# Attention beside a linear branch on one core: the keys' normaliser put on the values, the first 512 tokens turned by TensorE, 130 instead of 128 packs of exponentials off ScalarE

## The chip, the cores and the metric

One core of one Trainium2 chip. The metric is the device time of one execution in microseconds (us), as the median of several runs.

## The reference, cut to what matters

```python
# x [1, 2048, 512], H = 32 heads, Dh = 16; all inputs bf16
def branch_A(x, wqkv, wo):                      # softmax attention
    q, k, v = heads(x @ wqkv)
    p = softmax(q @ k.T * Dh ** -0.5)
    return merge(p @ v) @ wo

def branch_B(x, wqkv, w_phi, wo):               # linear attention
    q, k, v = heads(x @ wqkv)
    pq, pk = q @ w_phi, k @ w_phi               # per head, 16 x 16
    phi_q = concat(softmax(pq), softmax(-pq))   # 32 features
    phi_k = concat(softmax(pk), softmax(-pk))
    kv, z = phi_k.T @ v, phi_k.sum(over the tokens)
    o = (phi_q @ kv) / (phi_q @ z + 1e-6)
    return merge(o) @ wo

g = sigmoid((x * gate_w).sum(-1))
out = g * branch_A(x, A_wqkv, A_wo) + (1 - g) * branch_B(x, B_wqkv, B_w_phi, B_wo)
```

## The kernel before

Everything stays in SBUF; tokens are turned once into `xT` (512 features on the partitions, 2048 tokens along the free axis). A **group** `g` is one chunk `qc` of 512 queries and one of eight sets `g8` of four heads, of the 32, and it runs over the 16 tiles `kt` of 128 keys. One group and one key tile are a **pack** of four **units**, one for each head: a unit is the score matrix of one head, 128 keys by 512 queries, made by one matmul of 32 rows (L1022). There are 32 x 16 = 512 packs, 2048 units.

Most units have their exponential taken by ScalarE (ACT): `_exp` (L1070) reads two or three units in turn (1024 or 1536 columns) from a ring of five PSUM banks and writes bf16 into one of 30 slots of `ET`; the `k`-th scores wait for exponential `k - 2`, whose banks they use. `_pv` multiplies a pack's four tiles by the values (L1135, four column tiles of TensorE side by side) and adds them up in a PSUM bank over the 16 key tiles.

The other packs go **away** from ACT: `AWAY` holds five bits for each group, and each bit set takes one of five key tiles (1, 4, 7, 10, 13) of that group. For such a pack VectorE (DVE) turns each unit's scores into the bits of a bf16 power of two (`_vector_bits`, L940, 512 columns a time), two more terms of the same bits are made by adding a shift on DVE (`_vector_terms`, L962, for two packs at a time with 4096 columns, or a single one with 2048) and a third on POOL (`_pool_term`, L977, two for each pack), and all four terms are multiplied by the values (`vc` is the values times a factor). So a pack away costs ACT nothing, and TensorE four value products where the others take one.

Branch B and the projections run beside this. `_b_fuse` folds `w_phi` into the weights. For the keys (`_b_quad` with `s = 1`, four **quads** of four token tiles) DVE evicts the features' logits (L1279), takes maxima and minima over the 16 features by a tree, subtracts them, ACT takes the exponentials of both signs (L1308), DVE sums them, and `_b_scale` takes one reciprocal of all 256 sums (L1329) and multiplies both halves of the features (L1330, twice). `_b_v` projects branch B's values and copies them from PSUM into `VB` with a column of ones behind every four heads (L1266), and `_b_kv` multiplies features by values and adds into `kvacc` (260 columns: 4 x 65). The queries' quads follow (`s = 0`: two reciprocals' worth of work as a ratio, L1334 to L1336), then the products with `kvbd` and the output projections. The query branch needs only the ratio of its two sums, because one common factor per token and head cancels in `num / den`.

The order of the work is not written by hand. Every piece is an `Op` on an engine with a planned cost, a priority `prio` and sometimes an earliest place `rel`, and `Plan.order` builds, ahead of time, one fixed queue for each engine by simulating them; `emit` turns the dependences into semaphore waits. `SHIFT` is a table of tags ("e3" for the projection of values in `_b_v` of tile 3, "d4" a quad, "p101" a pack) with an offset added to that tag's priority. On the chip each engine follows its queue in order and waits where a semaphore isn't there yet.

The start: SP issues DMA transposes of `x` (`_turn`, L1390; first two halves of 256 tokens, then three chunks of 512), ACT's queue issues three pieces of the weights (L525). TensorE meanwhile runs nine matmuls on a constant tile (`_warm`, L639). Then come k of the first 256 tokens (L662), q of both halves (L713, evicted twice with a mask by DVE, L719), k of the other half, the first scores and the first exponential. At the end the last packs' values, their normalisation, the output projection and the store follow the last exponential.

Of the kernel before, what the change touches and what calls it, by code (L numbers as in the profile page):

```python
# [6 lines left out]
ACT = mybir.ActivationFunctionType  # L7
# [3 lines left out]
P = 128  # L11
D = 512
H = 32
DH = 16
# [372 lines left out]
class _Kernel:  # L387
# [43 lines left out]
    def _memory(self, ctx):  # L431
# [42 lines left out]
        self.VB = sb("VB", [P, 4, 8, 65], BF16)  # L474
# [5 lines left out]
        self.kvacc = sb("kvacc", [P, 2, 260], F32)  # L480
# [29 lines left out]
    def _loads(self):  # L510
# [18 lines left out]
        for half in range(2):  # L529
            load_x(0, QCH // 2 * half, QCH // 2 * (half + 1), 4.1)  # L530
            self.b_x0[half].writers = self.b_xT[0].writers[half:]
# [17 lines left out]
    def _consts(self):  # L549
# [20 lines left out]
        self.o_vbones = op("POOL", lambda e: e.memset(self.VB[:, :, :, 64:65], 1.0), 0.3, prio=-20)  # L570
# [25 lines left out]

    def _projections(self):
# [11 lines left out]
        self._warm(9)  # L609
# [25 lines left out]
    def _warm(self, n):  # L635

        def run(e):
            for _ in range(n):
                ins = e.matmul(self.ps[:, 4, :], self.warm[:, 0:P], self.warm, start=True, stop=True)  # L639
            return ins  # L640
        self.plan.op("PE", run, 0.427 * n, reads=[self.b_warm], name="warm", prio=-99)
# [63 lines left out]
    def _proj_q0(self, half, bank):  # L705
# [41 lines left out]
    def _gate(self):  # L747
# [44 lines left out]
    AWAY = (22, 27, 28, 19, 26, 15, 29, 27, 27, 15, 15, 30, 31, 13, 15, 27, 15, 23, 31, 27, 27, 31, 31, 31, 26, 31, 25, 31, 30, 15, 19, 31)  # L792

    SHIFT = (
# [752 lines left out]
```

## Time and profile before

| what | us |
|---|---|
| median of 3 runs (lowest, highest) | 743.38 (743.01, 743.54) |
| profiled execution, its own time | 743.37 |
| its span | 741.6 |
| busy: PE, DVE, ACT, POOL | 710.9, 693.9, 727.0, 279.7 |

The span is the time from the first to the last instruction of the profile; the execution's own time also holds what lies around it. PE is TensorE, PEld its weight loads, DVE is VectorE, SP the engine that issues most DMAs. L1070 is line 1070 of the kernel. The row of a group of instructions gives its count, its busy time in total, the mean time of one in ns, and the idle time of the engine ahead of it with what ended it. A row of waits gives the total, the number of times and the longest. A row of the chain gives start, length and what ran. Matmul times are modelled, so a busy TensorE isn't one at its peak.

### The profile page before, as it was taken

What the parts mean: (1) busy time and instruction counts of PE and PEld (TensorE: products, weight loads), DVE (VectorE), ACT (ScalarE), POOL (GpSimd) and SP (SyncE); (2) the same over time, 40 slices, a digit from 0 to 9 for tenths busy, and PEclk for the clock granted to TensorE, in tenths of its full rate; (3) what the DMA queues carried; (4) which work ended last, traced back from release to release, by engine and by line L of the source; (5) the groups of instructions that cost most, each with busy time, mean ns of one, the idle gap of its engine ahead of it and who ended that gap; (6) DMA issues with size and microseconds to landing.
All of it is one profiled execution on the core that took longest, in us unless ns stands there. A gap on an engine that the chain in (4) does not pass through costs nothing.

```text
span 741.6 us, 19810 instructions
## 1 busy us (share of the span) xinstructions
PE 710.9 (96%) x8580; PEld 232.8 (31%) x8599; DVE 693.9 (94%) x1097; ACT 727.0 (98%) x635; POOL 279.7 (38%) x277
## 2 busy tenths in 40 slices
PE   8999999999999999999998999999999999999998
PEld 4334333333232322322222223322323233322322
DVE  5889989988999999999999999999999999999996
ACT  6999999999999999999999999999999999999996
POOL 4631331423434335232434344245342433325342
PEclk9999999999999999999999999999999999999999
DMA  9400000000000010000101301131211320231110
GB/s 201 142 12 14 12 2 13 13 4 13 14 9 11 3 22 8 9 9 8 16 8 20 55 14 32 30 76 13 31 23 30 51 44 8 39 81 20 23 23 30
DMA packets 90040, 21.96 MB, mean 30 GB/s; under 512 B 82912, under 2 KB 89440, under 8 KB 89952
## 3 DMA queue, kind: packets, MB, share of 16 engines
q1 hardware_dynamic: 88224, 20.17, 14.5%
q8 instruction: 67, 1.10, 0.6%
q10 hardware_dynamic: 1728, 0.52, 0.3%
q14 instruction: 21, 0.17, 0.1%
HBM read 4.21 MB, written 2.10 MB: 9 GB/s over the span
## 4 chain that ended last, share of the span: by engine, by line
ACT 89%; PE 6%; DVE 2%; DMA 1%; SPq 0%; issue 0%; DVEq 0%
ACT ET L1070 85%; ACT bq L1308 4%; PE ps L1022 2%; PE ps L1135 2%; PE ps L646 2%; DVE va L940 1%; DVE vp L962 1%; DMA xT<-in_A_x_dram 1%; DMA WT<-nb 1%; PE ps L736 0%; DVE bq L1279 0%; DVE nb L1420 0%; SPq L1390 0%; ACT xT L1496 0%; DVE rb L1418 0%
## 5 line engine op out<-in xcount | busy, mean ns | idle before, releaser
L1070 ACT ACTIVATE ET<-ps 128x1536 bf16<-128x1536 f32 x615 | 699.8, 1372 | 5.2 <-PE ps L1022 4.9
L977 POOL TENSOR_SCALAR vp<-va 128x1024 uint16<-128x1024 uint16 x260 | 271.8, 1045 | 450.4 <-DVE va L940 137.7
L940 DVE TENSOR_SCALAR va<-ps 128x512 uint16<-128x512 f32 x512 | 335.2, 684 | 25.1 <-PE ps L1022 22.0
L1022 PE MATMUL ps<-qT,kT 32*128 32x512 bf16 x2048 | 311.6, 384 | 20.3 <-ACT ET L1070 15.9
L1022 PEld LDWEIGHTS ps<-qT,kT 32*128 32x128 bf16 x2048 | 81.0, 91 | 265.9 <-ACT ET L1070 165.3
L962 DVE TENSOR_SCALAR vp<-va 128x4096 uint16<-128x4096 uint16 (+1 forms) x143 | 159.4, 1123 | 0.6 <-PE ps L1135 0.4
L1135 PE MATMUL ps<-ET,V 128*32 128x512 bf16 x1536 | 148.4, 385 | 1.4 <-DVE T L1156 1.3
L1135 PE MATMUL ps<-vp,vc 128*32 128x512 bf16 x1024 | 93.3, 384 | 0.3 <-DVE vp L962 0.3
L646 PE MATMUL ps<-WB,xT 128*32 128x512 bf16 x768 | 57.9, 382 | 0.0
L1135 PEld LDWEIGHTS ps<-ET,V 128*32 128x32 bf16 x1536 | 39.3, 95 | 57.1 <-issue 40.7
L1142 PE MATMUL ps<-kT,zero 128*32 128x512 bf16 x552 | 50.1, 385 | 0.4 <-ACT ET L1070 0.3
L1135 PE MATMUL ps<-va,V 128*32 128x512 bf16 x512 | 50.2, 385 | 0.0
L1135 PE MATMUL ps<-vp,V 128*32 128x512 bf16 x512 | 47.1, 384 | 0.7 <-DVE vp L962 0.7
L646 PE MATMUL ps<-xT,WA 128*32 128x512 bf16 x480 | 36.1, 382 | 0.3 <-DVE va L940 0.3
L1135 PEld LDWEIGHTS ps<-vp,vc 128*32 128x32 bf16 x1024 | 24.4, 95 | 35.9 <-issue 24.9
L1308 ACT ACTIVATE bq<-bq 128x2048 bf16<-128x2048 bf16 x16 | 32.7, 2046 | 0.0
L1156 DVE STREAM_TRANSPOSE T<-ps 128x512 f32<-128x512 f32 x32 | 22.7, 709 | 1.7 <-PE ps L1135 1.7
L646 PE MATMUL ps<-WoA,onTA 128*32 128x512 bf16 x256 | 23.2, 383 | 0.0
L646 PE MATMUL ps<-WoB,WT 128*32 128x512 bf16 x256 | 23.0, 383 | 0.0
L1279 DVE CAST bq<-ps 128x512 bf16<-128x512 f32 x32 | 21.8, 683 | 1.1 <-PE ps L646 1.1
L646 PEld LDWEIGHTS ps<-WB,xT 128*32 128x32 bf16 x768 | 15.6, 95 | 19.0 <-issue 11.2
L1135 PEld LDWEIGHTS ps<-va,V 128*32 128x32 bf16 x512 | 13.3, 95 | 20.4 <-issue 16.6
(86 smaller groups left out, 357.9 us busy)
## 6 DMA issues: line engine op xcount, KB each, us to landing
turned<-T SPq DMA_DIRECT2D x240, 8.0 KB, 1.8
qT<-qs SPq DMA_DIRECT2D x120, 16.0 KB, 1.8
WB<-in_B_wqkv_dram SPq DMA_DIRECT2D x1, 1536.0 KB, 6.9
out_dram<-WB SPq DMA_DIRECT2D x12, 128.0 KB, 1.9
WA<-in_A_wqkv_dram SPq DMA_DIRECT2D x3, 384.0 KB, 6.1
WoA<-in_A_wo_dram SPq DMA_DIRECT2D x1, 512.0 KB, 7.9
WoB<-in_B_wo_dram SPq DMA_DIRECT2D x1, 512.0 KB, 8.8
WA<-in_A_wqkv_dram ACTq DMA_DIRECT2D x3, 128.0 KB, 3.6
```

The costliest lines, as they stand in the source:

```text
L646: ins = e.matmul(out[32 * g:32 * g + 32], lhs[:, 32 * g:32 * g + 32], rhs, start=start, stop=stop, tile_position=(0, 32 * g), skip_group_c ...
L940: parts.append(op("DVE", lambda e, j=j, job=job: e.tensor_scalar(self.va[:, pair, side, j, :], self._bank(job), SCALE * LOG2E * 128.0, (12 ...
L962: self.plan.op("DVE", lambda e, k=k, shift=shift: e.tensor_scalar(flat(self.vp[:, k]), flat(self.va[:, pair]), float(shift), None, op0=ALU ...
L977: o = self.plan.op("POOL", lambda e, flat=flat: e.tensor_scalar(flat[0], flat[1], 1.0, float(shift), op0=ALU.mult, op1=ALU.add), 0.08 + n ...
L1022: return e.matmul(out, self.kT[32 * i:32 * i + 32, cp, kt * TOK:(kt + 1) * TOK], self.qT[32 * i:32 * i + 32, s, :], start=True, stop=True, ...
L1070: o = plan.op("ACT", lambda e: e.activation(self.ET[:, a % NS:a % NS + n, :], self.ps[:, self._ring(a):self._ring(a) + n, :], ACT.Exp, sca ...
L1135: ins = e.matmul(self._bank(ot)[32 * i:32 * i + 32, :], V[:, v0:v0 + 32], tile(), start=(kt == 0), stop=(kt == self.NT - 1), tile_position ...
L1142: ins = e.matmul(self._bank(ot)[32 * i:32 * i + 32, :], self.zero[:], self.kT[:, 0, 0:QCH], start=False, stop=False, tile_position=(0, 32 ...
L1156: self.turned_out = op("DVE", lambda e: e.transpose(T1[:, side].rearrange("p b s -> p (b s)"), src()), 0.635, deps=last, writes=[b_T1[side ...
L1279: [lambda e, b, k=k: e.tensor_copy(bq[:, k].rearrange("p (g s v) -> p g s v", g=8, s=2)[:, :, 0, :], b.rearrange("p (g v) -> p g v", g=8))],
L1308: op("ACT", lambda e, side=side: e.activation(sides[side], sides[side], ACT.Exp, scale=1.0 - 2 * side), self.c_act(2048) + 0.04, reads=[bu ...
```

## The change

1. **Keys' normaliser.** For the keys' quads the sums of the negative side get one reciprocal (128 columns), written straight into the 17th column of each head in `VB` (now 8 x 68 columns a tile, 17 for each head). A ratio of the two sums and a second reciprocal scale the positive features alone (one L1330-like product instead of two). The eviction of the values in `_b_v` becomes a product with that column, which takes the place of the ones; it, its matmuls and the `kv` products now wait for the new buffer `b_vr`, and the value projections are due later (`GAP * 10.2` into the quad). `kvacc` has 272 columns.
2. **First tokens.** The first 512 tokens come by four plain loads into `ET` slots 20 to 23 and are turned by TensorE (`_first_tokens`): four transposes for each 128 tokens, copied from PSUM into `xT` by DVE (first and third) and ACT (second and fourth). The warming matmuls go from nine to four, with one more after the second and the fourth turn. The masked q of the second half for one side is evicted by ACT instead of DVE.
3. **130 packs.** `AWAY` has 130 bits set instead of 128, in other places, and `SHIFT` is another table.

The diff, with the table `SHIFT` and lines around left out:

```diff
--- before.py
+++ after.py
@@ -471,13 +471,13 @@
-        self.VB = sb("VB", [P, 4, 8, 65], BF16)
+        self.VB = sb("VB", [P, 4, 8, 68], BF16)
...
-        self.kvacc = sb("kvacc", [P, 2, 260], F32)
+        self.kvacc = sb("kvacc", [P, 2, 272], F32)
@@ -526,9 +526,8 @@
-        for half in range(2):
-            load_x(0, QCH // 2 * half, QCH // 2 * (half + 1), 4.1)
-            self.b_x0[half].writers = self.b_xT[0].writers[half:]
+        self.x0 = [self.dma("SP", f"x{t}", lambda e, t=t: e.dma_start(
+            self.ET[:, 20 + t], self.x2d[TOK * t:TOK * t + TOK, :]), cost=0.45, prio=-60 + t, lat=2.3) for t in range(4)]
...
-        self.o_vbones = op("POOL", lambda e: e.memset(self.VB[:, :, :, 64:65], 1.0), 0.3, prio=-20)
...
+    def _first_tokens(self):
+
+        op = self.plan.op
+        for t in range(4):
+            job, pool = self._job(t if t < 2 else None)
+
+            def turn(e, t=t, job=job):
+                for c in range(4):
+                    ins = e.transpose(self._bank(job).bitcast(BF16)[:, P * c:P * c + P], self.ET[:, 20 + t, P * c:P * c + P], self.iden[:])
+                return ins
+            m = op("PE", turn, 4 * self.c_pe(128), reads=[self.b_iden], deps=[self.x0[t]], name="xtr", prio=-90 + t,
+                   acquire=pool)
+            if t % 2:
+                self._warm(1, [m])
+            out = self.xT[:, :, TOK * t:TOK * t + TOK]
+            src = lambda job=job: self._bank(job).bitcast(BF16)[:, 0:QCH].rearrange("p (c j) -> p c j", c=4)
+            if t % 2:
+                o = op("ACT", lambda e, out=out, src=src: e.activation(out, src(), ACT.Copy), self.c_act(QCH), deps=[m],
+                       name="xtr_ev", prio=-90 + t, release=pool)
+            else:
+                o = op("DVE", lambda e, out=out, src=src: e.tensor_copy(out, src()), self.c_dve(QCH), deps=[m],
+                       name="xtr_ev", prio=-90 + t, release=pool)
+            if pool is None:
+                self.early[t] = o
+            self.b_x0[t // 2].writers.append(o)
+        self.b_xT[0].writers = self.b_x0[0].writers + self.b_x0[1].writers
+
...
-        self._warm(9)
+        self._warm(4)
+        self._first_tokens()
...
-    def _warm(self, n):
+    def _warm(self, n, deps=()):
 
         def run(e):
             for _ in range(n):
                 ins = e.matmul(self.ps[:, 4, :], self.warm[:, 0:P], self.warm, start=True, stop=True)
             return ins
-        self.plan.op("PE", run, 0.427 * n, reads=[self.b_warm], name="warm", prio=-99)
+        self.plan.op("PE", run, 0.427 * n, reads=[self.b_warm], deps=deps, name="warm", prio=-99)
 
...
-            o = op("DVE", lambda e, side=side: e.tensor_scalar(
-                self.qT[:, side, at], self._bank(job)[:, 0:QCH // 2], self.mask[:, side:side + 1], None, op0=ALU.mult),
-                self.c_dve(256), reads=[self.b_mask], deps=[m], name="qproj_ev", prio=-40 + 70 * side,
-                release=pool if side else None)
+            if half and not side:
+                o = a = op("ACT", lambda e: e.activation(
+                    self.qT[:, 0, at], self._bank(job)[:, 0:QCH // 2], ACT.Copy, scale=self.mask[:, 0:1]),
+                    self.c_act(256), reads=[self.b_mask], deps=[m], name="qproj_ev", prio=-40)
+            else:
+                o = op("DVE", lambda e, side=side: e.tensor_scalar(
+                    self.qT[:, side, at], self._bank(job)[:, 0:QCH // 2], self.mask[:, side:side + 1], None,
+                    op0=ALU.mult), self.c_dve(256), reads=[self.b_mask], deps=[m, a if half else None], name="qproj_ev",
+                    prio=-40 + 70 * side, release=pool if side else None)
...
-    AWAY = (22, 27, 28, 19, 26, 15, 29, 27, 27, 15, 15, 30, 31, 13, 15, 27, 15, 23, 31, 27, 27, 31, 31, 31, 26, 31, 25, 31, 30, 15, 19, 31)
+    AWAY = (29, 29, 22, 13, 15, 27, 19, 23, 31, 15, 15, 31, 25, 23, 31, 15, 23, 27, 27, 15, 23, 23, 31, 31, 21, 31, 30, 31, 23, 15, 13, 31)
 
     SHIFT = (
...
     )
 
...
-        self.b_brec = B()
+        self.b_brec, self.b_vr = B(), B()
...
         for t in range(0, NT, 4):
             due = self.K0 + self.SK * t
+            of(f"d{t}", self._b_quad, 1, t, due)
             for k in range(4):
-                of(f"e{t + k}", self._b_v, t + k, due + self.GAP * k)
-            of(f"d{t}", self._b_quad, 1, t, due)
+                of(f"e{t + k}", self._b_v, t + k, due + self.GAP * 10.2 + k)
             of(f"a{t}", self._b_kv, t, due + 12 * self.GAP)
...
     def _b_v(self, t, due):
-        if t < 4:
-            self.b_VB[t].writers = [self.o_vbones]
+        heads = self.VB[:, t % 4].rearrange("p g (i v) -> p (g i) v", v=17)
         self._proj(lambda c: self.xT[:, c, TOK * t:TOK * t + TOK], lambda c: self.WB[:, c, 2 * D:3 * D],
-                   [self.b_xT[t // 4], self.b_WB],
-                   [lambda e, b: e.tensor_copy(self.VB[:, t % 4, :, 0:64], b.rearrange("p (g v) -> p g v", g=8))],
-                   self.c_dve(512), due + 4, due - 3, "bv", [self.b_VB[t % 4]])
+                   [self.b_xT[t // 4], self.b_WB, self.b_vr],
+                   [lambda e, b: e.tensor_tensor(heads[:, :, 0:16], b.rearrange("p (h d) -> p h d", d=DH),
+                                                 heads[:, :, 16:17].to_broadcast([P, 32, DH]), ALU.mult)],
+                   self.c_dve(512), due, due - 3, "bv", [self.b_VB[t % 4]])
 
...
+        pos, neg, r = total[:, 0::2], total[:, 1::2], r[:, 0:32]
         if s:
-            half = [slice(0, 32), slice(32, 64)]
-            return [("b_rec", 1.66, self._low(lambda e: e.reciprocal(r, total)), tree, b_r)] + [
-                ("b_mul", two(2048), lambda e, h=h: e.tensor_tensor(x[:, h], x[:, h], spread(r[:, h], 32), ALU.mult),
-                 b_r + both, both if h.start else [Buf()]) for h in half]
-
-        pos, neg, r = total[:, 0::2], total[:, 1::2], r[:, 0:32]
+            col = self.VB[:].rearrange("p t g (i v) -> p (t g) i v", v=17)[:, :, :, 16]
+            return [("b_rec", 0.86, self._low(lambda e: e.reciprocal(col, neg)), tree, [self.b_vr]),
+                    ("b_ratio", 0.2, lambda e: e.tensor_tensor(pos, pos, col, ALU.mult), tree + [self.b_vr], tree),
+                    ("b_rec", 0.86, self._low(lambda e: e.reciprocal(r, pos)), tree, b_r),
+                    ("b_mul", two(2048), lambda e: e.tensor_tensor(x[:, 0::2], x[:, 0::2], spread(r, 32), ALU.mult),
+                     b_r + both, [both[0]])]
+
...
-                        ins = e.matmul(self._bank(job)[:, 65 * g4:65 * g4 + 65],
+                        ins = e.matmul(self._bank(job)[:, 68 * g4:68 * g4 + 68],
...
-            m = op("PE", mm, 16 * self.c_pe(65), reads=self.b_bq[0:2] + self.b_VB, name="kv", prio=due, acquire=job)
+            m = op("PE", mm, 16 * self.c_pe(68), reads=self.b_bq[0:2] + self.b_VB + [self.b_vr], name="kv", prio=due, acquire=job)
...
-            acc = self.kvacc[:, hf, :].rearrange("p (g v) -> p g v", g=4)
+            acc = self.kvacc[:, hf, :].rearrange("p (g i v) -> p g i v", g=4, i=4)
...
```

More of the change, by code (lines that the diff above doesn't have):

```diff
@@ L1357, in mm @@
                 return ins
-            m = op("PE", mm, 16 * self.c_pe(65), reads=self.b_bq[0:2] + self.b_VB, name="kv", prio=due, acquire=job)
+            m = op("PE", mm, 16 * self.c_pe(68), reads=self.b_bq[0:2] + self.b_VB + [self.b_vr], name="kv", prio=due, acquire=job)
             acc = self.kvacc[:, hf, :]
             if t == 0:
-                op("DVE", lambda e, acc=acc, job=job: e.tensor_copy(acc, self._bank(job)[:, 0:260]), self.c_dve(260),
+                op("DVE", lambda e, acc=acc, job=job: e.tensor_copy(acc, self._bank(job)[:, 0:272]), self.c_dve(272),
                    deps=[m], writes=[self.b_kv[hf]], name="kvacc", prio=due, release=job)
             else:
-                op("DVE", lambda e, acc=acc, job=job: e.tensor_tensor(acc, acc, self._bank(job)[:, 0:260], ALU.add),
-                   self.c_dve(260), deps=[m], reads=[self.b_kv[hf]], writes=[self.b_kv[hf]], name="kvacc", prio=due,
+                op("DVE", lambda e, acc=acc, job=job: e.tensor_tensor(acc, acc, self._bank(job)[:, 0:272], ALU.add),
+                   self.c_dve(272), deps=[m], reads=[self.b_kv[hf]], writes=[self.b_kv[hf]], name="kvacc", prio=due,
                    release=job)
```

4 lines of the change are left out of this document (2 added, 2 removed), and 200 rows, old and new, of the table SHIFT.

## The prediction

> **What bounds the kernel now.** I read the engine totals first, then what ScalarE waited for, then the chain of waits at both ends of the run.
>
> ```profile
> span 741.6 us, 19810 instructions
> ## 1 busy us (share of the span) xinstructions
> PE 710.9 (96%) x8580; PEld 232.8 (31%) x8599; DVE 693.9 (94%) x1097; ACT 727.0 (98%) x635; POOL 279.7 (38%) x277
> ```
>
> Three engines are over 90% busy, so the totals alone don't name the bound. What ScalarE (ACT) waited for does:
>
> ```profile
> ACT ET L1070 <- PE ps L1022: 4.9, 2, 4.7
> ACT xT L1496 <- PE ps L646: 4.2, 1, 4.2
> ACT L1070 <- issue: 2.3, 1, 2.3
> ACT ET L1070 <- PE ps L1135: 0.2, 1, 0.2
> ```
>
> This is the whole list. The 4.7 is the wait for the first scores, the 4.2 the wait before the last two evictions; in between ACT was held up for some 0.4 us in all. The chain of waits at the start, and the row of the timeline with the last exponentials:
>
> ```profile
> 0.74 1.35 SPq L1390
> 2.14 4.49 DMA xT<-in_A_x_dram
> 6.67 0.61 PE ps L713 x4
> 7.29 0.44 PE ps L662 x4
> 7.95 0.35 PE ps L1022 x3
> 8.32 31.77 ACT ET L1070 x28
> 40.19 72.52 ACT ET L1070 x64
> ```
>
> ```profile
> 725.05 8.38 ACT L1070 ACTIVATE ET<-ps 128x1024 bf16<-128x1024 f32 x8
> ```
>
> So the run has three parts: a start of 8.32 us (the second half of the first 512 tokens lands at 6.63, its q projection, masking and first scores follow), a gapless file of ACT work from 8.32 to 733.43, and a tail of 8.2 us to 741.6. The profiled execution took 743.37, that is 1.77 outside the span; the median of the three runs is 743.38, so profile and median agree and I sum against 743.37. A change shortens the run by what it takes off the start, off ACT's own work, or off the tail; DVE and PE count only where they make ACT wait.
>
> **ACT's work: fewer exponentials.** The counts of ones in the two AWAY tuples of the diff are 128 and 130 packs; a pack is four units of 128x512 scores. ACT keeps 4 x (512 - 128) = 1536 units before, 1528 after, in alternating instructions of three and two units.
>
> ```profile
> L1070 ACT ACTIVATE ET<-ps 128x1536 bf16<-128x1536 f32 x307 | 486.2, 1584 | 5.2 <-PE ps L1022 4.9 <-PE ps L1135 0.2
> L1070 ACT ACTIVATE ET<-ps 128x1024 bf16<-128x1024 f32 x307 | 357.0, 1163 | 0.0
> L1308 ACT ACTIVATE bq<-bq 128x2048 bf16<-128x2048 bf16 x16 | 32.7, 2046 | 0.0
> L1070 ACT ACT_TABLE_LOAD x1 | 1.3, 1283 | 2.3 <-issue 2.3
> L1496 ACT ACTIVATE xT<-ps 128x512 bf16<-128x512 f32 x2 | 1.1, 596 | 4.2 <-PE ps L646 4.2
> L1070 ACT ACTIVATE ET<-ps 128x512 bf16<-128x512 f32 x1 | 0.7, 707 | 0.0
> ```
>
> The means 1584 and 1163 overlap with their neighbours (their sum is 2.75); what a pair really takes is its pitch, 72.52 / 32 = 2.266 us by the longest piece of the chain. Before: 307 pairs and one single unit, 307 x 2.266 + 0.71 = 696.4. After: 1528 = 305 x 5 + 3, so 305 pairs and a last instruction of three, 305 x 2.266 + 1.58 = 692.7. **Saved: 3.7 us.** The sixteen L1308 stay. The two evictions of the first tokens and one masked q that move to ACT stand ahead of the first exponential, where ACT idles anyway.
>
> **The start.** Gone are two DMA transposes; instead SP issues four plain loads of 128 tokens (128 KB each), TensorE turns each in four 128x128 transposes into PSUM, and DVE (tokens 0 and 2 of the four groups) or ACT (1 and 3) copies it out. Nothing before shows that load, so I bound it by two issues of the same size:
>
> ```profile
> WA<-in_A_wqkv_dram ACTq DMA_DIRECT2D x3, 128.0 KB, 3.6
> out_dram<-xT SPq DMA_DIRECT2D x3, 128.0 KB, 1.9
> ```
>
> ```profile
> 0.74 1.55 ACTq L525 DMA_DIRECT2D WA<-in_A_wqkv_dram  x3
> ...
> 1.45 4.02 PE L639 MATMUL ps<-bq 128*128 128x512 bf16 x9 [1.45 <-DVE bq L572]
> ```
>
> The weights land 3.6 us after issue, cut into 256-byte pieces and beside other loads; the stores of whole 1 KB rows land after 1.9 in a quiet stretch. The new loads have the rows of the second and the crowd of the first: I take 2.5. At 1.55 / 3 = 0.52 per issue the fourth is issued at 0.74 + 3 x 0.52 = 2.3 and lands at 4.8 (4.2 to 5.9 by the two rows). Its turn is half as many columns as the four matmuls of L662 (0.44), at most 0.4 with its way to PSUM; its copy by ACT is L1496's shape, 0.6; two semaphores, 0.1. The last q projection (L713 at 6.67) then starts at 5.9, 0.8 earlier. Ahead of it on PE stand the k and q projections of the first 256 tokens, 0.44 each: the second load lands at 1.26 + 2.5 = 3.8, is turned and copied by 4.9, and both are through by 5.8, just in time. From L713 to the first exponential it took 8.32 - 6.67 = 1.65; the masking on that way goes from DVE to ACT with about the same price, so I keep 1.65. **First exponential at 7.55, saved 0.8**; by the bounds from 1.4 saved to 0.3 lost. SP's three other transposes of x come up behind 2.1 us of issues instead of two L1390 issues (0.74 to about 3.5), so 0.7 earlier: the later tokens move up with the start and nothing there is newly late.
>
> **DVE, PE and POOL: what fills up behind ACT.** Normaliser of the keys, four quads:
>
> ```profile
> L1329 DVE RECIPROCAL brec<-bsum x4: 1733/1744/1746, 128.4 to 343.3; 128x256 f16<-128x256 f32 x4
> L1334 DVE RECIPROCAL bsum<-bsum x4: 943/948/949, 401.1 to 653.9; 128x128 f32<-128x128 f32 x4
> L1335 DVE TENSOR_TENSOR brec<-bsum x4: 230/282/286, 403.1 to 655.3; 128x128 f16<-128x128 f32 x4
> ```
>
> ```profile
> L1330 DVE TENSOR_TENSOR bq<-bq,brec x8: 1206/1216/1221, 135.4 to 348.4; 128x2048 bf16<-128x2048 bf16 x8
> ```
>
> ```profile
> L1364 DVE TENSOR_TENSOR kvacc<-kvacc,ps x6: 421/424/426, 220.8 to 352.3; 128x260 f32<-128x260 f32 x6
> L1361 DVE COPY kvacc<-ps x2: 414/420/427, 141.8 to 144.0; 128x260 f32<-128x260 f32 x2
> ```
>
> One reciprocal of 256 and two multiplications (1.74 + 2 x 1.22 = 4.18) become two reciprocals of 128, a ratio and one multiplication (2 x 0.95 + 0.28 + 1.22 = 3.40): 0.78 less per quad, 3.1 in all. The values' eviction becomes a product; L1364 against L1361 shows that a second operand beside PSUM costs 4 ns, so nothing. Twelve more columns in kvacc: under 0.1 in all. The two new packs:
>
> ```profile
> L940 DVE TENSOR_SCALAR va<-ps 128x512 uint16<-128x512 f32 x512 | 335.2, 684 | 25.1 <-PE ps L1022 22.0
> L962 DVE TENSOR_SCALAR vp<-va 128x4096 uint16<-128x4096 uint16 x111 | 137.3, 1241 | 0.2
> ...
> L962 DVE TENSOR_SCALAR vp<-va 128x2048 uint16<-128x2048 uint16 x32 | 22.4, 711 | 0.4 <-PE ps L1135 0.4
> ```
>
> ```profile
> L977 POOL TENSOR_SCALAR vp<-va 128x1024 uint16<-128x1024 uint16 x260 | 271.8, 1045 | 450.4 <-DVE va L940 137.7 <-DVE vp L962 115.5 <-PE ps L1135 94.2
> ```
>
> Eight more L940 are 5.5; the groups go from 56 pairs and 16 singles to 58 and 14, with two terms each on DVE: 4 x 1.24 - 4 x 0.71 = 2.1. So DVE gains 7.6 and loses 3.1, **4.5 us more on DVE** (its two copies at the start and the masking that it gives up lie ahead of the first exponential's file and about cancel). POOL gets four more L977 (4.2 us of an engine at 38%). PE gets 24 more value matmuls, little beside the 15.9 us that it waits for ACT:
>
> ```profile
> PE ps L1022 <- ACT ET L1070: 15.9, 43, 0.8
> ```
>
> Where the quads of the keys lie, DVE has this room:
>
> ```profile
> 88.00:190.00 102.00, 99.47 (x1291) 36.40 (x1289) 93.36 (x146) 101.84 (x89) 30.46 (x30) 1.00 0.05 9
> 190.00:330.00 140.00, 133.36 (x1623) 41.02 (x1619) 136.59 (x205) 140.00 (x122) 52.12 (x50) 1.00 0.06 11
> ```
>
> (stretch, length, then busy of PE, PEld, DVE, ACT, POOL.) DVE idles 8.6 and 3.4 us here: 12 us for 4.5. I cost the DVE work at nothing on that cover; without it, up to 4.5. The tail keeps its steps; I take it unchanged, half a microsecond either way.
>
> **Sum:** 743.37 - 3.7 - 0.8 = **738.9 us**.
>
> **Rivals.**
>
> *The start is not won.* The nine warming matmuls ran back to back for 4.02 us, 0.45 each; the four 256-column matmuls of L662 (0.44, so 0.22 for 512 columns) ran twice as fast. The change leaves four, and one after every second turn. If PE is then still at the slow pace, the k, q and q projections take about 0.85 instead of 0.44 each, the first scores 0.2 more, and the exponential starts 1.2 later than forecast, at 8.75: 740.1. For it: a gap wherever a load is late. Against: four warmers fill 1.45 to 3.2, about when the first load lands (0.74 + 2.5). The Trainium skill (TensorE: Matmul & The Clock Gate, Part 1) puts the change of pace at some 3.4 us of sustained activity counted in a free-running window; by that rule fewer warmers with gaps start the projections cold and the sum would be the rival's 740.1. The trace agrees with a change of pace after some 4 us of warmers and does not show what gaps do. The same time comes from a second table load (1283 ns) between the first copies and the first exponential; one load served Exp and L1496's copy, so I hold it unlikely. The Trainium skill (ScalarE: Activation LUTs, Table sets) says that cheap functions such as copy stand in every set, so a set chosen for the first copy need not hold Exp. Chance 0.14.
>
> *DVE becomes the bound.* Its idle time may be no room: it mostly waits for scores, which the order on PE brings when it brings them. Then the 4.5 us come back into ACT's file in part or whole: 741 to 743.4. Against: ACT waited 0.4 us in 725 with DVE 98% busy from 190 to 330. Chance 0.13, a third of it still faster.
>
> *Slower: PE stands still for the normaliser.* The V projections of branch B now wait for the new reciprocal (b_vr), and the kv matmuls for V. PE's queue is in order, so while it waits the scores of the next exponential stand behind it, then ACT. The cover is short: an exponential of two units holds ACT 0.92 of the pitch, the scores need 0.35, about 0.5 is left. Decisive is whether DVE runs more than 0.5 behind the place that the order gave it: one pair term (1.24) is 0.74 too late. Three such waits among the four V projections and two kv products of each quad, in all four quads, are 12 x 0.74 = 8.9: 747.8; from two per quad on (738.9 + 5.9 = 744.8) the gain is gone. For it: a new dependence of PE on DVE in DVE's fullest stretch. Against: the before run holds evictions of the same kind with ACT gapless. Chance 0.11.
>
> **How the numbers follow.** Forecast 0.62 (738 to 739.7), lost start 0.14, DVE bound 0.13, normaliser 0.11. A measurement of this kernel can tell some 0.2% from no change, 1.5 us, that is 741.9 and 744.9. Faster: 0.62 + 0.14 + 0.04 = 0.80; same: 0.09; slower: 0.11. The range runs from 737.8 (best landing, tail 0.4 shorter) to 742.5 (half or more of the DVE rival); outside stay the slower case, the top of the DVE rival (0.06) and 0.02 below.
>
> **What would show it.** Right: 611 L1070 instructions, the first at about 7.6; ACT's waits after it under 1 us in all; DVE near 698; a tail of 8 us; projections of the first tokens at 0.44 for four. Wrong: ACT waiting for PE in pieces of 0.3 us and more around the key quads (PE held by DVE's reciprocal), a first exponential past 8.3, or a second table load.

## The result, and the profile after

| | us |
|---|---|
| before, median of 21 runs (lowest, highest) | 743.54 (742.81, 744.50) |
| after, median of 21 runs (lowest, highest) | 744.94 (742.88, 749.21) |
| ratio after to before, 95% interval | 1.0019 (1.0010 to 1.0028) |
| after, profiled execution; its span | 744.98; 743.2 |

The change, forecast at 738.9, made the kernel 0.2% slower. The page's totals and the whole list of ScalarE's waits, after:

```profile
span 743.2 us, 19756 instructions
PE 713.2 (96%) x8543; PEld 235.0 (32%) x8562; DVE 697.0 (94%) x1110; ACT 725.2 (98%) x634; POOL 283.4 (38%) x280
```

```profile
ACT ET L1101 <- PE ps L1053: 4.7, 9, 1.3
ACT xT L1529 <- PE ps L672: 3.9, 1, 3.9
ACT xT L612 <- PE ps L603: 2.8, 2, 1.6
ACT L612 <- issue: 2.4, 1, 2.4
ACT qT L746 <- PE ps L739: 0.9, 1, 0.9
ACT ET L1101 <- PE ps L1166: 0.2, 1, 0.2
```

The three rows of L612 and L746 lie ahead of the first exponential. But the first row is a new one: before, 4.7 of its 4.9 was the one wait for the first scores; now it is nine waits, of which only 0.58 us is the wait for the first scores; 3.3 us of the rest lie between 60 and 80 us, inside the unbroken row of exponentials (the file). ScalarE's timeline at both ends:

```profile
7.03 0.60 ACT L612 ACTIVATE xT<-ps 128x512 bf16<-128x512 bf16 x1 [1.60 <-PE ps L603]
8.55 0.47 ACT L746 ACTIVATE qT<-ps,mask 128x256 bf16<-128x256 f32 x1 [0.93 <-PE ps L739]
9.61 1.45 ACT L1101 ACTIVATE ET<-ps 128x1536 bf16<-128x1536 f32 x1 [0.58 <-PE ps L1053]
...
733.88 1.46 ACT L1101 ACTIVATE ET<-ps 128x1536 bf16<-128x1536 f32 x1
```

The first exponential starts at 9.61 instead of 8.32 (forecast 7.55), the last ends at 735.34. The account of the profiled run: 743.37, + 1.3 for the start, + 0.6 for the file (725.7 instead of 725.1 although it should be 3.7 shorter), - 0.3 for the tail (743.2 - 735.34 = 7.9 instead of 8.2) = 745.0. So two things are to be explained: the start, and some 4 us inside the file.

The start, on TensorE:

```profile
3.32 0.58 PE L603 MATMUL ps<-iden,ET 128*128 128x128 bf16 x4
4.18 0.60 PE L603 MATMUL ps<-iden,ET 128*128 128x128 bf16 x4 [0.29 <-DMA ET<-in_A_x_dram]
5.74 0.40 PE L603 MATMUL ps<-iden,ET 128*128 128x128 bf16 x4 [0.72 <-DMA ET<-in_A_x_dram]
6.59 0.40 PE L603 MATMUL ps<-iden,ET 128*128 128x128 bf16 x4 [0.46 <-DMA ET<-in_A_x_dram]
7.04 0.60 PE L688 MATMUL ps<-xT,WA 128*128 128x256 bf16 x4
7.48 1.04 PE L739 MATMUL ps<-xT,WA 128*128 128x256 bf16 x8
```

```profile
DMA to landing us min/median/max: 2.4/3.5/4.4
```

(the second is the line on the four loads of L529.) The last load lands 4.4 us after its issue, in time for a turn at 6.59: as late as the second DMA transpose did before (6.63). The turn and its copy come on top.

Inside the file the loss has a place. The windows of two microseconds around 70 us (length, busy of PE, PEld, DVE, ACT, POOL, then the granted TensorE clock; the last two columns are DMA's):

```profile
64.00:66.00 2.00, 1.81 (x26) 0.61 (x23) 2.00 (x4) 2.00 (x3) 0.06 (x1) 1.00 0.01 1
66.00:68.00 2.00, 1.55 (x16) 0.47 (x14) 1.91 (x5) 2.00 (x3) 0.98 (x1) 1.00 0.00 0
68.00:70.00 2.00, 1.12 (x11) 0.55 (x11) 1.94 (x5) 1.45 (x3) 1.04 (x1) 0.89 0.03 8
70.00:72.00 2.00, 1.94 (x15) 1.31 (x16) 1.97 (x4) 1.32 (x2) 0.00 (x0) 0.50 0.00 0
72.00:74.00 2.00, 2.00 (x18) 1.37 (x17) 1.42 (x4) 0.69 (x1) 0.00 (x0) 0.50 0.00 0
74.00:76.00 2.00, 2.00 (x18) 1.08 (x22) 1.67 (x3) 1.91 (x2) 0.00 (x0) 0.50 0.00 0
76.00:78.00 2.00, 2.00 (x34) 0.55 (x22) 0.45 (x2) 1.27 (x2) 0.00 (x0) 0.91 0.04 4
```

Read the rows downwards: VectorE is full, TensorE gets less and less to do (1.81, 1.55, 1.12), and ScalarE stands for the first time in this stretch, for 0.55 us up to 69.54. From 69.54 on the clock is halved (half pace), for 6.8 us, and ScalarE waits three times more (0.68, 1.34 and 0.72 us). Before, the same stretch has a clock of 1.00 and ScalarE at 2.00 in every window, for example:

```profile
68.00:70.00 2.00, 2.00 (x22) 0.84 (x20) 1.72 (x4) 2.00 (x3) 0.00 (x0) 1.00 0.13 12
```

That first wait came before the clock fell, so the two prices have to be told apart: what the lack of work costs, and what the half pace adds. What VectorE and GpSimd do there:

```profile
65.77 0.68 DVE L1287 CAST WB<-ps 128x512 bf16<-128x512 f32 x1
66.37 1.03 DVE L815 COPY ghb<-gh 32x16 f32<-32x16 f32 x3
67.43 0.69 DVE L971 TENSOR_SCALAR va<-ps 128x512 uint16<-128x512 f32 x1
68.04 0.68 DVE L1287 CAST WB<-ps 128x512 bf16<-128x512 f32 x1
68.75 0.53 DVE L815 COPY ghb<-gh 32x16 f32<-32x16 f32 x1
69.31 1.29 DVE L1287 CAST WB<-ps 128x512 bf16<-128x512 f32 x2
```

```profile
65.94 1.04 POOL L1008 TENSOR_SCALAR vp<-va 128x1024 uint16<-128x1024 uint16 x1 [5.82 <-DVE va L971]
68.20 1.04 POOL L1008 TENSOR_SCALAR vp<-va 128x1024 uint16<-128x1024 uint16 x1 [1.22 <-DVE va L971]
```

The four L815 are copies of 32 x 16 numbers for the gate (L784 before). The new order has put them among the evictions of the first of the two weight folds (L1287; the second fold's evictions run at 85.8 to 90.1), which TensorE waits for. The kernel before had them together ahead of its second fold. Their durations, before and after:

```profile
L784 DVE COPY ghb<-gh x4: 151/166/171, 62.1 to 62.7; 32x16 f32<-32x16 f32 x4
```

```profile
L815 DVE COPY ghb<-gh x4: 165/346/635, 66.4 to 68.8; 32x16 f32<-32x16 f32 x4
```

Two of the four are long, 635 and 526 ns, and they end at 67.00 and 69.28, within 0.04 us after the two GpSimd instructions (65.94 + 1.04 and 68.20 + 1.04). The two in between, with GpSimd idle, take 165 and 167. So a copy seems to wait until GpSimd is through.

### The profile page after: what moved, and what is told of

Its sections match the earlier page's. It is cut to its first block, busy times and chain, and to the rows that moved or that the text cites. A ratio compares the mean times of both kernels' runs of the same rounds, so it can differ in the third digit from the quotient of the medians.

```text
span 743.2 us, 19756 instructions
## 1 busy us (share of the span) xinstructions
PE 713.2 (96%) x8543; PEld 235.0 (32%) x8562; DVE 697.0 (94%) x1110; ACT 725.2 (98%) x634; POOL 283.4 (38%) x280
## 4 chain that ended last, share of the span: by engine, by line
ACT 59%; PE 33%; DVE 6%; DMA 1%; issue 1%; SPq 0%
ACT ET L1101 56%; PE ps L1053 12%; PE ps L1166 11%; PE ps L672 5%; DVE va L971 3%; ACT bq L1339 3%; PE ps L767 1%; PE ps L1173 1%; DVE vp L993 1%; PE ps L1445 1%; DMA ET<-in_A_x_dram 1%; PE ps L1074 0%; DVE nb L1453 0%; DVE T L1187 0%; DVE WB L1287 0%
## 5 line engine op out<-in xcount | busy, mean ns | idle before, releaser
L1008 POOL TENSOR_SCALAR vp<-va 128x1024 uint16<-128x1024 uint16 x264 | 275.7, 1044 | 448.3 <-DVE vp L993 165.0
L971 DVE TENSOR_SCALAR va<-ps 128x512 uint16<-128x512 f32 x520 | 339.8, 682 | 23.9 <-PE ps L1053 20.6
L1173 PE MATMUL ps<-kT,zero 128*32 128x512 bf16 x468 | 42.2, 385 | 0.0
L767 PE MATMUL ps<-WA,xT 128*128 128x128 bf16 x256 | 21.5, 232 | 0.6 <-DVE WB L1287 0.6
L672 PE MATMUL ps<-WoA,onTA 128*32 128x512 bf16 x256 | 21.7, 382 | 0.2 <-DVE onTA L1203 0.2
```

Of the source, the lines that this page charges most:

```text
L672: ins = e.matmul(out[32 * g:32 * g + 32], lhs[:, 32 * g:32 * g + 32], rhs, start=start, stop=stop, tile_position=(0, 32 * g), skip_group_c ...
L767: ins = e.matmul(self._bank(job)[:, P * tt:P * tt + P], self.xT[:, c, QCH * j + TOK * tt:QCH * j + TOK * tt + TOK], self.WA[:, 2, c, P * c ...
L971: parts.append(op("DVE", lambda e, j=j, job=job: e.tensor_scalar(self.va[:, pair, side, j, :], self._bank(job), SCALE * LOG2E * 128.0, (12 ...
L1008: o = self.plan.op("POOL", lambda e, flat=flat: e.tensor_scalar(flat[0], flat[1], 1.0, float(shift), op0=ALU.mult, op1=ALU.add), 0.08 + n ...
L1173: ins = e.matmul(self._bank(ot)[32 * i:32 * i + 32, :], self.zero[:], self.kT[:, 0, 0:QCH], start=False, stop=False, tile_position=(0, 32 ...
```

## The experiments

The fourteen kernels keep the queues of the changed kernel (e9: those of the kernel before) and edit them after they are built, so that the order stays the same but for the edit. The edits are shown in short, not as literal code. They ran in four groups, with medians of the kernel before of 743.22, 743.22, 743.17 and 743.31.

**e1: the changed kernel again.**

> The changed kernel once more, to see whether the half-pace stretch of TensorE at 69.5 to 76.4 us recurs and where. Theory A (the new order starves TensorE around 65 to 70 us and the clock gate answers): again a stretch at 0.50 granted clock that begins between 66 and 75 us, ACT losing 2.5 to 4 us there; median 744.5 to 745.5. Rival B (the stretch is a chance event of that one execution): none, or elsewhere, and the median then is near 742. In both the first exponential starts at 9.2 to 9.9.

745.24 (743.32 to 746.61), ratio 1.0025 (1.0016 to 1.0034). The profiled run, with 743.32 the fastest of twelve, shows another accident than the first profile: no half pace near 70 us (ScalarE lost 0.9 there, with two copies as long as before, 635 ns at most), but TensorE still at half pace at the projections, and a first exponential at 11.03. In this trace's clock record full clock begins only at 9.42 us, in the first profile at 4.69:

```profile
7.54 1.06 PE L688 MATMUL ps<-xT,WA 128*128 128x256 bf16 x4
8.39 1.54 PE L739 MATMUL ps<-xT,WA 128*128 128x256 bf16 x8
```

The eight L739 take 1.54 us here, 1.04 in the profile shown above. That one profile can't tell whether the half pace near 70 us recurs; the mean granted clock of each run can. At 743 us a mean of 0.998 stands for some 3 us at half pace, 0.995 for some 7. It is 0.998 or less in 17 of 21 runs of the changed kernel and in 10 of 12 of e1, in none of the kernel before beside e1 (34 runs). So it recurs in most runs, though this mean does not say where in the run.

**e2: the gate's five small instructions later on VectorE**, 40 places behind the last fold's last eviction.

```diff
+ at = rest.index(last_fold_eviction) + 40
+ queue["DVE"] = rest[:at] + gate + rest[at:]
```

> Same queues, but the five small DVE instructions of the gate (L815, L819) stand some 40 instructions later on DVE, so they no longer lie among the weight-folding evictions at 66 to 70 us. Theory A with DVE crowding as its cause: TensorE gets its folded banks 1.0 to 1.7 us earlier, the half-pace stretch goes or is rarer, ACT's waits after the start fall from 4.3 to under 1.5, median 741.5 to 743. Rival C (the stretch comes from too few matmuls in the queue there, whatever DVE does): no change, 744.5 to 745.5.

742.70 (741.18 to 743.83), ratio 0.9991 (0.9982 to 1.0000): 2.5 less than e1. The copies, now at 113 us, take 152 to 171 ns; ScalarE waits nowhere between 60 and 80 us, and the mean clock is 0.999 or 1.000 in all eleven runs.

**e3: three filling groups of four matmuls ahead of each of four L1282**, so that TensorE is not idle there.

```diff
+ if o.name == "wphi" and seen < 4:  out += 3 * [pad]
```

> Same queues with three more filling groups of four matmuls (0.22 us a group) ahead of each of the four folding products L1282 at 65 to 69 us. Theory A (clock gate): TensorE stays at full pace, granted clock 1.00 from the first exponential on, ACT's waits in 60 to 80 us fall from 3.3 to under 1 (the fillers themselves can cost up to 0.6), median 741.5 to 743. Rival D (ACT is starved by DVE directly and the pace is only a side effect): ACT still loses 2 to 4 us there, 744 to 746.

745.23 (743.55 to 746.54). The clock stays up, the time is not won:

```profile
66.00:68.00 2.00, 2.00 (x27) 0.71 (x28) 1.56 (x5) 1.86 (x2) 1.05 (x1) 1.00 0.03 8
68.00:70.00 2.00, 2.00 (x30) 0.87 (x32) 1.39 (x4) 1.49 (x2) 1.05 (x1) 1.00 0.00 0
70.00:72.00 2.00, 2.00 (x29) 0.97 (x21) 1.57 (x5) 0.64 (x1) 0.00 (x0) 1.00 0.00 0
```

TensorE is busy to 2.00 at clock 1.00, and ScalarE stands all the same (1.49, 0.64). The mean clock is 1.000 in all eleven runs. So a clock that stays up is not enough. But the fillers take TensorE's own time as well (here 1.9 us of ScalarE's is lost between 60 and 80 us, in e1 without them 0.9), so this run does not give the price of the half pace. The profile of e6, further down, does so better: its four copies are as long as in the changed kernel (637 ns at most), its clock stays at 1.00, and ScalarE loses 0.8 instead of 3.3:

```profile
66.00:68.00 2.00, 1.38 (x14) 0.61 (x14) 1.91 (x5) 2.00 (x3) 0.78 (x2) 1.00 0.00 0
68.00:70.00 2.00, 1.24 (x16) 0.77 (x15) 1.94 (x4) 1.46 (x2) 0.71 (x1) 1.00 0.00 0
```

**e4: DMA transposes and nine warming matmuls as before** (the masked q stays on ScalarE).

```diff
- four loads, four turns, their copies, 4 + 1 + 1 warming matmuls
+ two dma_start_transpose, 9 warming matmuls
```

> Same queues, but the first 512 tokens come by two DMA transposes as before, nine warming matmuls, no turn on TensorE and no copies; the masked q stays on ACT. Theory A (turn and copy are added behind a landing that the bytes in flight set, some 6.5 us either way): first exponential at 8.3 to 8.5 instead of 9.6, 1.1 to 1.3 us off the time if all else stays; the half-pace stretch may stay, so 743.2 to 744.4, or 741 without it. Rival E (something else in the start is late, for example the weights): first exponential stays past 9.2.

743.13 (742.25 to 743.54), 2.1 less than e1, though the first exponential of its profile comes no earlier, at 9.65:

```profile
7.30 1.28 ACT L746 ACT_TABLE_LOAD   x1 [7.30 <-PE ps L739]
8.60 0.47 ACT L746 ACTIVATE qT<-ps,mask 128x256 bf16<-128x256 f32 x1
```

With the copies gone, the masked q is ScalarE's first instruction, and the table load that stands ahead of it waited for the q projections with it: 1.28 us on the path. In the changed kernel, and in the kernel before, that load ran at 2.3 us beside the loads. So the expected time came, but not by the expected earlier exponential: where the 2.1 us come from is not shown. (None of e4's runs has a mean clock below 0.997, five of e1's have 0.995, which can be a part of it.)

**e6: the start of the kernel before in full** (e4, and the masked q on VectorE).

> The start of the kernel before in full, nothing else. Theory: first exponential at 8.3 to 8.4 against 9.65 in the variant with the start partly undone, the half pace near 70 us stays; 743.13 - 1.3 = 741.8. Rival (TensorE's and VectorE's load at 60 to 80 us meets ScalarE earlier, since their work there is bound to loads and not to ScalarE): an earlier ScalarE waits longer there, 743.1.

741.39 (740.69 to 742.54), ratio 0.9975 (0.9967 to 0.9984); first exponential at 9.05 (8.3 to 8.4 was expected). 3.9 less than e1. Its five runs with a mean clock of 0.998 or less have a median of 742.09, the seven others 741.07: about 1 us for the half pace in this kernel.

**e5: e6 and e2 together.**

> The start of the kernel before in full (transposed loads, nine warming matmuls together, masked q on VectorE) in the changed kernel, and the five small gate instructions of the gate later on VectorE. Theory (two losses, each on its own: start 1.3 us, crowding of VectorE at 64 to 70 us 2.5 to 3.3 us): first exponential at 8.3 to 8.4, no half pace near 70 us, ScalarE loses under 1 us at 60 to 80 us; 742.70 of the gate variant less 1.2 = 741.5. Rival A (the two are one: what the early start gives is waited for later): 742.7. Rival B (the end becomes the bound: output projections wait for a transposing DMA near 716 us, and ScalarE comes to it earlier still): the wait grows from 1.6 to 2.8 and 742.5 stands.

739.70 (739.44 to 740.25), ratio 0.9954 (0.9942 to 0.9967). The two losses are separate and about add up: 745.24 - 2.5 - 3.9 = 738.8 (measured 739.70; the expected 741.5 counted only 1.2 for the start). The feared wait at the end is not there, and the first exponential is at 9.09, not at 8.3 to 8.4. This is the change with its second part (the first tokens) undone and the copies moved: 3.5 below the kernel before and, with e10 and e12, the fastest version.

**e7: e2, and half of V's weights asked for behind the four loads of x.**

```diff
- queue["ACT"]: dma wa2, first half
+ queue["SP"], behind x3: dma wa2, first half
```

> The changed kernel with the gate later and with the first half of V's weights asked for behind the four loads of x instead of beside them. Theory (the last 128 tokens land at 6.55 because 512 KB of x share the DMA engines with 384 KB of weights): with a third less in flight they land at 5.6 to 5.8, the first exponential comes at 8.6 to 8.8 and the time is 742.70 - 0.8 = 741.9. Rival (the loads' landing is set by the issue and latency of each, not by what else is in flight): landing 6.5, first exponential 9.55, 742.7.

741.01 (739.84 to 742.30), 1.7 less than e2. The loads land after

```profile
DMA to landing us min/median/max: 2.2/3.1/3.6
```

```profile
5.30 1.03 PE L603 MATMUL ps<-iden,ET 128*128 128x128 bf16 x8 [0.31 <-DMA ET<-in_A_x_dram]
```

so the third and the fourth turn now run in one go and end at 6.33 instead of 6.99, in a run in which TensorE was at half pace until 7.27. What else is in flight does move the landing: the slowest of the four loads takes 4.1 to 4.6 us in the five profiles with that piece beside them (after, e1, e2, e3, e13), 3.6 and 3.5 in the two with it behind (e7, e14). But the 1.7 us can't be put down to it. The first exponential comes at 9.48 here, not at 8.6 to 8.8, and at 9.55 in e2; what the two profiles differ by is a wait of 1.60 us near the end of e2's, shown further down.

**e9: the kernel before, with its gate copies among the second fold's evictions.**

> The kernel before with nothing changed but VectorE's order: its gate instructions stand among the second fold's evictions, as in the changed kernel, instead of together ahead of them. Theory (that order alone feeds TensorE too slowly): a stretch at half pace near 70 us, ScalarE loses 1 to 3 us there more than before, 744.2 to 746. Rival (the order matters only together with the later start or the multiplication of keys' values): 743.2, no half pace.

743.58 (742.86 to 744.76), ratio 1.0005 (0.9997 to 1.0014): the rival. The copies take 154 to 171 ns there, and GpSimd is idle from 59.6 to 72.37. This is the second fold of the kernel before, not the first as in the changed kernel, but at the same time of the run (68.1 to 69.5). There a place among the evictions alone costs nothing that can be measured; my theory of mere crowding was wrong, and the collision with GpSimd became the next one.

**e10: e6, with the four copies as reductions over an axis of one element, at the same place.**

```diff
- e.tensor_copy(ghb[32i:32i+32], src[:, :, i])
+ e.tensor_reduce(ghb[32i:32i+32], src[:, :, i:i+1], AX.X, ALU.add)
```

> The variant with the start of the kernel before (741.39) and the gate's four small copies where the changed kernel has them, but each as a reduction over an axis of one element: same data, same place, another kind of VectorE instruction. In the changed kernel two of the four copies took 635 and 526 ns and ended with a GpSimd instruction (L1008) that had begun before them; the other two took 165. Theory (a plain copy from SBUF waits until GpSimd's instruction is through, a reduction does not): all four at about 0.2, VectorE 0.8 us further at 70 us, and of the 1.7 us that moving the gate gave at least half: 739.9 to 740.6. Rival (the length belongs to the place, behind a full eviction, and any instruction there has it): durations and 741.4 stay.

739.91 (739.60 to 740.58), 1.5 less than e6 and equal to e5, where the gate was moved. VectorE's and GpSimd's timelines, to be held against those above:

```profile
65.15 0.56 DVE L1570 TENSOR_REDUCE ghb<-gh 32x16 f32<-32x16 f32 x3
...
67.06 0.18 DVE L1570 TENSOR_REDUCE ghb<-gh 32x16 f32<-32x16 f32 x1
```

```profile
64.72 1.05 POOL L1008 TENSOR_SCALAR vp<-va 128x1024 uint16<-128x1024 uint16 x1 [5.81 <-DVE va L971]
66.52 1.05 POOL L1008 TENSOR_SCALAR vp<-va 128x1024 uint16<-128x1024 uint16 x1 [0.75 <-DVE va L971]
```

All four run in the midst of a GpSimd instruction, and take 157 to 177 ns. The Trainium skill (SBUF — State Buffer, Who interferes with whom) says that a plain copy can run in a mode that needs a port pair shared with GpSimd and, where GpSimd's instruction was issued first, blocks until that one is over, and that a reduction never contends for it. The two profiles agree: 635 and 526 ns against 177 at most.

**e11: e6, with the gate ahead of the second fold's evictions.** The copies came to stand at 80.8 us. I had taken the fold at 64 to 70 us, among whose evictions the changed kernel has them, for the second; it is the first of two.

> The same base, the five gate instructions together just ahead of the first eviction of the second fold, as in the kernel before. GpSimd begins its first instruction of that stretch only about then. Theory of the collision: no copy over 200 ns, or one, time 739.9 to 740.6. Rival (any VectorE work ahead of the fold's evictions delays TensorE, collision or not): the five take 0.95 us in front of all four evictions instead of being spread among them, 741.4 or up to 742.2.

740.38 (739.98 to 740.77), copies of 152 to 172 ns. It is one more place away from GpSimd's two instructions, and it says nothing on a place just ahead of the first fold's evictions, which I had meant.

**e13: the changed kernel with the reductions alone.**

> The changed kernel with one edit: the gate's four small copies are reductions over an axis of one element, at the same place. Theory (two of the copies wait out a GpSimd instruction, and the 0.8 us of VectorE that this costs at its fullest is what leaves TensorE underfed and brings the half pace): no copy over 0.2 us, no half pace near 70 us, ScalarE loses under 1 us at 60 to 80 us; 745.2 less 2.0 to 2.5 = 742.7 to 743.2, the time of the variant with the gate moved. Rival (the collision mattered only together with the rest, the order of the fold alone underfeeds TensorE): half pace stays in most runs, 744.5 or more.

743.02 (740.73 to 745.70), ratio 0.9998 (0.9986 to 1.0010). 2.2 less than e1, within 0.3 of the variant with the gate moved: the collision is what that place costs the changed kernel. Its profile has a clock of 1.00 in all windows from 64 to 78 us, and eleven of its twelve runs a mean clock of 0.999 or more (10 of e1's twelve had less). The runs still spread by 5 us; e2, with the same start, spreads by 2.7, and where this spread comes from is not shown.

**e8: e5, and one more 2048-wide multiplication on VectorE in each quad of keys**, its result unused.

```diff
+ e.tensor_tensor(btree, btree, btree, ALU.mult)   # ahead of b_mul, four times
```

> The variant with the start of the kernel before and the gate later (739.70), and in each of the four quads of keys one more 2048-wide multiplication on VectorE (1.2 us each, 4.9 in all, its result used by nobody). Theory of the prediction (VectorE's idle time there is room, 12 us for 4.5): no change to 740.2, ScalarE waits under 0.5 more. Rival (VectorE's idle time is no room): 740.9 to 744.6.

743.26 (742.43 to 743.36): 3.6 more for 4.9 us of work. TensorE's waits between 160 and 250 us:

```profile
PE ps L672 <- DVE VB L1296: 0.8, 1, 0.8
PE ps L1053 <- DVE VB L1296: 0.5, 1, 0.5
```

These are waits for the values' product, which follows the new normaliser on VectorE; e5 has none of them there. Between 160 and 480 us ScalarE waits 2.1 us here and nowhere in e5; the rest of the 3.6 I have not located. In this stretch VectorE's idle time is no reserve: what the order did not plan for is paid at about three quarters.

**e12: e5, with V's weights behind x.**

> The variant at 739.70, and the first half of V's weights asked for behind the two transposing loads of x. Theory (bytes in flight set the landing of x): the second 256 tokens land 0.4 to 0.7 earlier than 6.7, first exponential 0.3 to 0.6 earlier, 739.2 to 739.4. Rival (the transposing loads take their 1.3 us of issue and 3.2 us of way whatever else is in flight): 739.7, or later by up to 0.5 where V's projections then wait for their weights ahead of scores on TensorE.

739.87 (739.46 to 740.22): no gain over e5, although the two transposing loads landed after 4.4 and 3.8 us instead of 4.5 and 4.2, so the theory missed. The profiled runs themselves, 739.46 and 740.23, differ by 0.8, as their first exponentials do (8.31 and 9.09); but in them full clock begins at 5.47 and 7.33 us, and that time scatters between runs of the same start (see below).

**e14: e7, with three warming matmuls instead of one behind the second turn.**

> The variant with the gate later and V's weights behind x (741.01), with three warming matmuls instead of one after the second turn, so that TensorE has no pause between 4.4 and 5.7 us. Theory (in part of the runs the pause keeps TensorE at half pace until past 9 us and costs 1.4 us): the slower half of the runs, 741.3 to 742.3, is gone; median 740.0 to 740.5. Rival (the two groups of runs come from the end, where a transposing DMA lands late or not): both groups stay, 741.0; if the warmers themselves delay the third turn, up to 741.4.

740.95 (739.76 to 741.05, five runs). No run is above 741.1, where half of e7's twelve were, but the median stays: not decided with so few runs.

## Why the prediction was wrong, point by point

**The start (the step "I take 2.5 ... lands at 4.8").** Wrong sign: forecast 0.8 earlier, found 1.3 later in the profile. The four loads landed after 2.4 to 4.4 us, the last beyond my upper row (3.6). I took the latency of one load and let all four have it; but 512 KB of x and 384 KB of weights were under way together, and e7 shows that with one piece of 128 KB less ahead of it the slowest takes 3.6. The old DMA transposes carried the same bytes in the same time, so beside these weights replacing them did not bring the last tokens earlier, and the turn and its copy (0.4 + 0.6) were added. My rival *the start is not won* had the right direction; of its mechanisms a second table load did not occur in the changed kernel, and TensorE still at half pace at the projections occurred in some profiles (e1, e13; for the first of them also in e5 and e6, behind nine warming matmuls). It had the size wrong because it kept my landing times.

Undoing the start is worth 3.0 (e2 to e5) to 3.9 us (e1 to e6). The profiles account for less than half: the first exponential starts at 9.55 to 11.03 in after, e1, e2, e3 and e13 (mean 10.0), and at 8.31 to 9.13 in the eight profiles with the start of before (mean 8.7). Inside each group it goes with the time at which the trace's clock record has full clock begin: with the start of before, 5.36 to 5.61 us for the three at 8.31 to 8.37, 6.25 and 6.36 for 8.69 and 8.73, 6.84 to 7.33 for the three at 9.05 to 9.13; with the four loads, 4.69 to 5.28 for the three at 9.55 to 9.74, 8.04 and 9.42 for 10.11 and 11.03. At an early full clock the difference is 1.3 as well. Of the larger figure, 3.9, a part is the half pace near 70 us, which e6 has less often than e1.

One profile, e2's, shows a further loss of that kind of start, at the end:

```profile
717.70 2.37 ACT L1101 ACTIVATE ET<-ps 128x1536 bf16<-128x1536 f32 x2 [1.60 <-PE ps L1053]
```

```profile
onTA<-turned SPq DMA_TRANSPOSE x1, 4.5
```

A transposing DMA of the last queries landed after 4.5 us (2.4 in e5, e7 and the changed kernel's profile), and TensorE, then ScalarE, waited for it. Fifteen of its sixteen parts were there by 714.30, the last at 716.47; a fetch of 16 KB of instructions had begun at 714.01. That the one held up the other is a guess from one run; it was not tried. The rest of those 3.0 to 3.9 us stays open.

**The new order (costed at nothing).** I costed the changed operations and took the order of everything else as neutral, though the change replaced the whole table of priorities. It moved four copies, 0.65 us of work, beside two GpSimd instructions; they grew to 1.5, VectorE was 0.8 late where it was fullest, TensorE ran out of work, its clock was halved in most runs, and 2.2 us were gone (e13). None of my rivals had it. It could not be read from the profile of before, but that the order was unknown could: it belonged into the range. The kernel's source had a hint: the program that builds the order keeps the VectorE operations named in `PORT` (L115) apart from GpSimd's, and the copies' name, `gate_b`, is not among them.

**ScalarE's work (-3.7).** Right. From the first exponential to the end of the last it took 725.1 before and, with the accidents taken out (e5), 721.5:

```profile
9.09 2.37 ACT L1101 ACTIVATE ET<-ps 128x1536 bf16<-128x1536 f32 x2 [5.47 <-PE ps L1053]
...
714.46 16.12 ACT L1101 ACTIVATE ET<-ps 128x1024 bf16<-128x1024 f32 x14
```

714.46 + 16.12 - 9.09 = 721.5. And e5's 739.70 against 743.22 is 3.5: with the two losses undone, this term of the sum is what is left of the forecast.

**VectorE at nothing, and the rival that it becomes the bound.** The forecast held for the order as built: VectorE went from 693.9 to 697.0 (3.1 more, 0.8 of it the collision, where I had 4.5), and ScalarE did not wait once between 160 and 340 us. But the reason was wrong. I called the 12 us of idle time a cover; e8 shows that 4.9 us more in the same place cost 3.6. Here what the order had planned was free, what came on top was not. The product with the normaliser costs nothing, as forecast: 675 ns (L1296) against 687 for the plain eviction (L1266).

**The slower rival, TensorE standing still for the normaliser.** Not seen after the change. It exists, though: e8's two waits of 0.8 and 0.5 are it. The kernel did become slower, by a smaller amount and by another mechanism.

**The tail.** Unchanged within the half microsecond given.

## What to carry to other kernels

A load's landing time can depend on all that is asked for at that moment (here 4.1 to 4.6 us against 3.5 to 3.6 with 128 KB less), so before replacing a slow-looking transfer add up what is in flight; here the bytes stayed, and so did the landing. When a change comes with a new order, the order is an edit of its own: look at which small instructions came to stand beside a GpSimd instruction on VectorE, and what waits behind them. Idle time of an engine in a full schedule need not be room for work that the schedule did not plan. And one profile of a start is one draw: look at several before believing half a microsecond.

## What the runs showed of the hardware that I had not expected

- A copy of 32 x 16 numbers from SBUF to SBUF on VectorE took 635 and 526 ns while GpSimd worked, 151 to 172 ns otherwise; the same as a reduction took 157 to 181 ns beside GpSimd (e10, e13).
- TensorE's clock was halved for 6.8 us after a few microseconds in which it was not idle but some 55 to 80% busy (1.12 and 1.55 of 2.00). The Trainium skill (TensorE: Matmul & The Clock Gate, Part 1) counts activity in windows of 3.4 us and speaks of an idle window before the clock falls; the length agrees with two such windows, while the busy share in the rows is far from idle. Nor does the busy share alone decide: in e1 and e6 windows of 1.38 and 1.24 of 2.00 kept the clock at 1.00.
- For the changed kernel full clock began 4.69 us after the start of one profiled run and 9.42 us after that of another (e1), and the first exponential came at 9.61 and 11.03.
- A table load waits with the instruction that it stands ahead of: 7.30 us in e4, 2.3 us where ScalarE's first instruction was another one.
